# Scores of two heads in one planned step, planner durations reset, and low weight halves moved from an adding DMA to VectorE

## The chip, the core and the metric

The kernel runs on one core of one Trainium2 chip: TensorE (PE; its weight loads are listed as PEld), VectorE (DVE), ScalarE (ACT), GpSimd (POOL), SyncE (SP, which issues most transfers) and 16 DMA engines. The metric is the device time of one execution in microseconds (us), as the median of the runs.

## What is computed

Four batches of eight heads, 576 positions of 64 numbers each, go through attention of two kinds whose results are added; two dense layers follow over 2304 tokens of 512 numbers.

```python
q_d, k_d, v_d = means of 4 neighbouring positions          # 144 rows a head
out_up    = repeat(softmax(q_d @ k_d.T / 8) @ v_d, 4)       # attention over the means
out_local = softmax(where(|i-j| < 4, q @ k.T / 8, -1e9)) @ v
x = (out_up + out_local) as (2304, 512)
x = leaky(x @ moe_w_in, 0.01) @ moe_w_out                   # 512 -> 2048 -> 512
g(h) = h if h >= 1; 0 if h <= -1; else (h + 1)**2 / 4
return g(x @ moe2_w_in) @ moe2_w_out
```

## The kernel before

**Dense layers.** Every matrix is kept as a sum of two float16 parts, a high and a low one, and a product is three matmuls (high by high, high by low, low by high). Tokens go in five blocks (512, 512, 512, 512, 256); hidden columns go in 16 chunks of 128. A *step* is one chunk: 12 matmuls of 128x512 for the first layer (`g1`, L1456), ScalarE and VectorE work that makes the two parts of the activation (`act_a` L1472 or L1476, `act_s` L1480, `act_g` L1484, `act_h` L1496, and `act_l`, L1500 on VectorE), then 12 matmuls for the second layer (`g2`, L1521 in the first dense net, L1533 in the second). The blocks run in `ORDER`: blocks 0 and 1 of net 1, 0 and 1 of net 2, 2 and 3 of net 1, and so on. L1500 runs once a step (with two chunks a step in the small block, 144 times), so the n-th L1500 marks a place in the program.

**Weights.** `weight` brings each of 64 chunks (32 for each net) as raw 8-byte words, turns them into float32 on VectorE (L565, L572, L579), rounds to the high part on ScalarE (L595) and makes the low part. For net 1 the low part is one VectorE instruction (L628). For net 2, `LO_DMA` sends it another way: ScalarE writes the negated high part (L616), a DMA issued by GpSimd adds it onto the float32 value (L619), and ScalarE rounds the sum (L623).

**Attention over the means.** `down(b, hp, due)` runs for a batch and a pair of heads, 16 chains in all. For batches 0 and 1 the means of q and k come from sums over loaded and transposed tiles; for batches 2 and 3 from loads, adding DMAs issued by GpSimd (L828), an addition on VectorE (L835) and transposes on PE (L865, L869). Then `scores(par)` (L878) makes 2 matmuls of 72x144 in float32 for each head `par` of the pair, into that head's own PSUM bank; `peak` (L892) and `pexp` (L900) follow; `rec`, `norm` (L919), transposes (L929, L937) and `av` (L947, L955) end the chain. In the trace a float32 matmul has two records, so one `scores(par)` shows as x4.

**Local attention.** Tokens 0 to 1023 go through PE (`local_p`: L1022, L1037, L1050, L1055, L1080, L1097, after `prep`, whose transposes are L755). The rest goes through VectorE (`local_d`, five units: L1232, L1240, L1277, L1307), with transposes L1313 at the end.

**The order.** Nothing is scheduled by hand. Every piece of work is an `Op` with an engine, an assumed duration, dependencies, SBUF need, PSUM banks and a key (a due step less a lead). `Issue.run` plays the whole program through on assumed durations: whenever an engine is free it emits the ready op of the lowest rank, so the durations decide the order in which each engine's instructions are written. On the chip each engine runs its list in that order and waits on semaphores. The dense layers hold six of the eight banks while they run. Until the first dense matmul, whenever PE would have nothing ready, the planner writes a matmul over zeros into its list (`fill`, L1658, 0.216 us by its own count); afterwards it writes none. `pe_tr` gives the assumed time of a set of transposes, `pe_mm` of a set of matmuls, `t_dve` and `t_act` of one instruction, and `lat` is the flight of a transfer.

Of the kernel before, what the change touches and what calls it, by code (L numbers as in the profile page):

```python
# [45 lines left out]
D_ACT = (0, 0)  # L46
D_ACT_OF = {3: (2, 2)}

LO_DMA = {1: (99, 99), 2: (0, 99)}


LO_PE = (0, 0)
# [267 lines left out]
def kernel(  # L320
# [11 lines left out]
    nc = tc.nc  # L332
    B, H, S, D = q.shape
# [62 lines left out]

    def pe_tr(n, k, rows):

        return dict(dur=k * (0.003 + 2 * n / 2400.0), cols=k * 2 * n * rows / 128.0)

    def pe_mm(dur, n, k, rows):

# [4 lines left out]

    STEP = 5.2
    DMA = 0.47


    ident = const.tile([P, P], F32, name="ident")
# [122 lines left out]
    def weight(m, which, f, due):  # L535
# [49 lines left out]
            st["s"].free()  # L585
            w_open[0] -= 1

        o = ch.op("SP", DMA, load, need=(1024,), lat=1.55)
        o.gate = lambda: w_open[0] < AHEAD and (
            m == 1 or w_begun[1] == 2 * KFF and o.key <= sch.step + WINDOW_W and arena.close_spare()  # L590
        )
# [116 lines left out]
    def prep(b, hp, due):  # L708
# [67 lines left out]
        ch.rush, ch.window = RUSH_B.get(b, RUSH), WINDOW_B.get(b, WINDOW_A)  # L776
        ld = {}
        for nm, src in (("q", q), ("k", k)):
            ld[nm] = ch.op("SP", 2 * DMA, lambda nm=nm, src=src: load(nm, src), [],
                           need=(QBB * P,), lat=1.85)  # L780
        last = {}
        for nm in "qk":
# [7 lines left out]
                          after=(lambda nm=nm, i=i: banks.put(st["ps", nm, i]),))  # L790
            last[nm] = c
        n_v = 1 + (b == hp == 0) + (b == B - 1 and hp == NHP - 1)
        last["v"] = ch.op("SP", n_v * DMA, load_v, [], need=(2 * QBB * D,), lat=1.8)
        ch.close()
        last["load"] = ld["k"]
        prep_ready[b, hp] = last
# [2 lines left out]
    def down(b, hp, due):  # L799
# [46 lines left out]

        for nm, src in (("v", v),) if from_t else (("q", q), ("k", k), ("v", v)):
            o = ch.op("SP", DMA, lambda nm=nm, src=src: load(nm, src), [], need=(4 * rw * D,),
                      lat=rw * 0.42)
            if from_t:  # L850
                raw_v = o
            if whole:
                o = ch.op("Pool", 1.25, lambda nm=nm, src=src: more(nm, src), [o])
            else:
                o = ch.op("Pool", 1.05, lambda nm=nm, src=src: more(nm, src), [o], lat=0.85)
            pooled[nm] = ch.op("DVE", t_dve(256), lambda nm=nm: total(nm), [o], need=(4 * D,),
                               after=(lambda nm=nm: st["r" + nm].free(),))
# [12 lines left out]

        s_e = 1.0 / 16.0 if from_t else 1.0 / 128.0

        def scores(par):
            qk = st["qkT"].ap.rearrange("p (a g) -> p a g", a=2)
            st["ps_s", par] = banks.get()
            pp = slice(par * D, (par + 1) * D)
            for a in range(2):
                nc.tensor.matmul(  # L878
                    psv(par)[:, a, :], qk[pp, 0, a * GH:(a + 1) * GH], qk[pp, 1, :],
                    start=True, stop=True,  # L880
                )

        def psv(par):
            return st["ps_s", par][:GH, :2 * G].rearrange("p (a g) -> p a g", a=2)
# [75 lines left out]
        if from_t:  # L960
            r = prep_ready[b, hp]
            o = ch.op("DVE", t_dve(S), lambda: total_t("q"), [r["q"]], need=(2 * G,),
                      after=(qT[b, hp].done,))
            ch.op("DVE", t_dve(S), lambda: total_t("k"), [r["k"], o], after=(kT[b, hp].done,))
        else:
            ch.op("PE", pe_tr(GH, 4, GH), qk_t, [pooled["q"], pooled["k"]], banks=1,
                  after=(lambda: st["q"].free(), lambda: st["k"].free()))
            ch.op("ACT", t_act(288, True), qk_c, need=(2 * G,),
                  after=(lambda: banks.put(st["ps_t"]),))
        o = ch.ops[-1]  # L970
        e, x = None, None
        for par in range(2):
            o = ch.op("PE", pe_mm(0.49, G, 2, D), lambda par=par: scores(par), [o], banks=1,
                      after=(lambda: st["qkT"].free(),) if par else ())
            e = ch.op("DVE", 0.56, lambda par=par: peak(par), [o, e], need=() if par else (8,))
            x = ch.op("ACT", 2 * t_act(G, True, 2), lambda par=par: pexp(par), [e, x],
                      need=() if par else (4 * G,),
                      after=(lambda par=par: banks.put(st["ps_s", par]),))
# [3 lines left out]
        else:  # L982
# [6 lines left out]
                   after=(lambda: st["p"].free(),))  # L989
        c1 = ch.op("ACT", t_act(288, True), lambda: p_c(1), [t1, c0],  # L990
                   after=(lambda: banks.put(st["ps_p", 1]),))
        ch.op("PE", pe_mm(0.5, G, 4, GH), av, [c0, c1, pooled["v"]], banks=1,
              after=(lambda: st["v"].free(), lambda: st["pT"].free()))
        o = ch.op("ACT", t_act(144, True), av_c, need=() if hp else (NHP * G,), main=True,
                  after=(lambda: banks.put(st["ps_o"]),))
# [9 lines left out]
    def local_p(b, n0, cnt, hp, due):  # L1005
# [119 lines left out]
        def xl():  # L1125
# [3 lines left out]
            )  # L1129

        r = prep_ready[b, hp]
        ch.op("PE", pe_mm(0.12 + 0.172 * cnt, KB, 2 * cnt, D), scores, [r["q"], r["k"]], banks=1,
              after=(qT[b, hp].done, kT[b, hp].done))
        ch.op("DVE", t_dve(cnt * KB), peak, need=(2 * cnt,))
        ch.op("ACT", cnt * t_act(KB, True, 2), pexp, need=(cnt * KB,),
# [34 lines left out]
    def local_d(u, due):  # L1170
# [202 lines left out]
        for par in range(2):  # L1373
            reds = []
            mul = None
            for j0 in range(0, L, JC):
                end = j0 + JC == L
                o = mul = ch.op(
                          "DVE", big, lambda par=par, j0=j0: qk_mul(par, j0),
                          [ld["q", par], ld["k", par], mul],  # L1380
                          need=(JC * W * D,) + ((L * W,) if j0 == 0 else ()),
                          after=freer(*([("q", par), ("k", par)] if end else [])))
                if (par, j0) in q_act:
                    o = on_act(qk_red_act, par, j0, [o])
                    o.after = freer(("prod", par, j0))
                else:
                    o = ch.op("DVE", big, lambda par=par, j0=j0: qk_red(par, j0), [o],
                              after=freer(("prod", par, j0)))
                reds.append(o)
            o = ch.op("DVE", 0.685, lambda par=par: soft1(par), reds, need=(L,))  # L1390
            ex[par] = ch.op("ACT", t_act(56), lambda par=par: nc.scalar.activation(
                out=sv(par), in_=sv(par), func=AF.Exp, scale=0.125), [o])
            nrm[par] = ch.op("DVE", 0.815, lambda par=par: soft2(par), [ex[par]],
                             after=freer(("m", par)))
        fin = []
        done = {}
        for jh, j0 in enumerate(range(0, L, JC)):
            last = []
            for par in (1, 0) if (0, j0) in v_act else (0, 1):
                end = j0 + JC == L  # L1400
                if (par, j0) in v_act:
                    o = on_act(av_mul_act, par, j0, [nrm[par], ld["v", par]],
                               need=(JC * W * D,))
                else:
                    o = ch.op("DVE", big, lambda par=par, j0=j0: av_mul(par, j0),
                              [nrm[par], ld["v", par]], need=(JC * W * D,))
                o = done[par] = ch.op("DVE", t_dve(JC * 3 * D) + t_dve(JC * 2 * D) + t_dve(JC * D),
                                  lambda par=par, j0=j0: av_red(par, j0),
                                  [o, done.get(par)],
                                  need=Need(lambda: "o" in st, L * 2 * D),  # L1410
                                  after=freer(("prod", par, j0),
                                              *([("v", par), ("s", par)] if end else [])))
                last.append(o)
# [282 lines left out]
```

## Time and profile before

| | us |
|---|---|
| median of 3 runs (lowest, highest) | 875.11 (872.43, 875.77) |
| the profiled execution: its own time | 877.15 |
| its span, first to last instruction | 875.3 |
| PE busy | 865.7 (99%) |
| VectorE busy | 539.1 (62%) |
| ScalarE busy | 419.1 (48%) |
| GpSimd busy | 72.4 (8%) |
| mean granted TensorE clock | 0.994 |

Busy time of PE is to be read with care: matmuls overlap in their pipeline, so a group's length is best read from its start to the start of the next one. The shares are means over very different stages; VectorE at 62% is full in some stretches and nearly idle in the last half. An instruction on VectorE shows some 0.08 us that already overlaps with the next when both stand close together.

### The profile page before, as it was taken

The numbers are of one execution on the slowest core, as the hardware profiler recorded it, in microseconds if no ns is written. First come the engines' busy times: TensorE is split into PE (matmuls) and PEld (weight loads), VectorE is DVE, ScalarE is ACT, GpSimd is POOL, SyncE is SP. The second block draws the span as 40 slices with busy tenths as digits, with TensorE's granted clock in tenths as the row PEclk, the third lists the DMA queues.
The fourth block names the chain that finished last, engine by engine and source line by source line (L and its number), as shares of the span: only waits on it lengthen the run. The fifth ranks groups of instructions, "written<-read, shape, count | busy, mean of one in ns | idle before, by whom it ended". The sixth has DMA issues, their size and how long they took to land.

```text
span 875.3 us, 13271 instructions
## 1 busy us (share of the span) xinstructions
PE 865.7 (99%) x5014; PEld 446.0 (51%) x5014; DVE 539.1 (62%) x943; ACT 419.1 (48%) x973; POOL 72.4 (8%) x96
## 2 busy tenths in 40 slices
PE   9999999999999999999999999999999999999998
PEld 5765554444444444454444444444444488544564
DVE  5878999776679998848988955951322211322221
ACT  4878775677766433554444323222433332434343
POOL 2111000122210031100420000000000000000000
PEclk9999999999999998999999999999999999999999
DMA  8999466699984173312662004000000010000010
GB/s 149 163 189 219 154 205 189 157 254 237 245 205 105 23 173 48 90 43 67 115 136 71 1 1 109 0 1 1 1 1 0 1 50 1 1 1 1 0 49 24
DMA packets 84973, 76.07 MB, mean 87 GB/s; under 512 B 36910, under 2 KB 70574, under 8 KB 84910
## 3 DMA queue, kind: packets, MB, share of 16 engines
q1 hardware_dynamic: 69102, 62.69, 26.8%
q0 software_dynamic: 15808, 12.54, 9.7%
q8 instruction: 39, 0.64, 0.3%
q14 instruction: 24, 0.20, 0.1%
HBM read 62.08 MB, written 4.72 MB: 76 GB/s over the span
## 4 chain that ended last, share of the span: by engine, by line
PE 65%; DVE 3%; DMA 2%; ACT 1%; issue 1%; POOL 0%; POOLq 0%; SPq 0%; ACTq 0%
PE bank L1456 31%; PE bank L1533 20%; PE bank L1521 12%; DMA arena<-in_k_dram 1%; PE bank L878 1%; DMA arena<-arena 1%; DVE arena L1240 1%; PE bank L929 1%; PE bank L947 1%; PE bank L1313 1%; DVE arena L1307 0%; DVE arena L1500 0%; PE bank L865 0%; DVE arena L835 0%; DVE arena L579 0%
## 5 line engine op out<-in xcount | busy, mean ns | idle before, releaser
L1456 PE MATMUL bank<-arena,w 128*128 128x512 f16 (+1 forms) x1920 | 395.6, 358 | 0.3 <-DVE arena L1561 0.3
L1456 PEld LDWEIGHTS <-w 128*128 128x128 f16 x1920 | 186.6, 98 | 182.8 <-issue 1.6
L1533 PE MATMUL bank<-w,arena 128*128 128x512 f16 x864 | 201.1, 383 | 0.4 <-ACT arena L1496 0.2
L1521 PE MATMUL bank<-arena,w 128*128 128x512 f16 (+1 forms) x960 | 200.3, 360 | 0.0
L1500 DVE SCALAR_TENSOR_TENSOR arena<-arena 128x512 f16<-128x512 f32 x144 | 99.0, 688 | 140.1 <-ACT arena L1496 137.8
L1521 PEld LDWEIGHTS <-w 128*128 128x128 f16 x960 | 93.3, 98 | 91.4 <-issue 3.5
L1533 PEld LDWEIGHTS <-arena 128*128 128x128 f16 x864 | 84.3, 98 | 100.1 <-issue 4.0
L1484 DVE SCALAR_TENSOR_TENSOR arena<-arena,bank 128x512 f32<-128x512 f32 x72 | 49.2, 684 | 134.0 <-ACT arena L1480 134.0
L1496 ACT ACTIVATE arena<-arena 128x512 f16<-128x512 f32 x144 | 90.6, 629 | 80.3 <-DVE arena L1484 73.3
L1476 ACT ACTIVATE arena<-bank,half 128x512 f32<-128x512 f32 x72 | 49.2, 684 | 119.4 <-PE bank L1456 117.5
L1472 ACT ACTIVATE arena<-bank 128x512 f32<-128x512 f32 x72 | 42.6, 592 | 120.1 <-PE bank L1456 119.8
L1480 ACT ACTIVATE arena<-arena 128x512 f32<-128x512 f32 x72 | 45.3, 629 | 1.9
L1307 DVE TENSOR_TENSOR arena<-arena 128x768 f32<-128x768 f32 (+2 forms) x60 | 41.2, 688 | 1.4
L619 POOL DMA_DIRECT2D arena<-arena x32 | 27.8, 869 | 160.9 <-DVE arena L565 70.1
L1232 DVE TENSOR_TENSOR arena<-arena 128x1792 f32<-128x1792 f32 x20 | 40.3, 2017 | 1.0 <-DMA arena<-in_k_dram 0.5
L1240 DVE TENSOR_REDUCE arena<-arena 128x28 f32<-128x1792 f32 x20 | 40.2, 2008 | 0.0
L1277 DVE TENSOR_TENSOR arena<-arena 128x1792 f32<-128x1792 f32 x20 | 40.1, 2014 | 0.0
L623 ACT ACTIVATE w<-arena 128x512 f16<-128x512 f32 x32 | 20.0, 626 | 19.2 <-DMA arena<-arena 19.0
L595 ACT ACTIVATE w<-arena 128x512 f16<-128x512 f32 x34 | 21.1, 621 | 10.6 <-DVE arena L579 10.6
L579 DVE SCALAR_TENSOR_TENSOR arena<-arena 128x512 int32<-128x512 int32 x32 | 22.1, 689 | 0.7
L572 DVE SCALAR_TENSOR_TENSOR arena<-arena 128x512 int32<-128x512 int32 x32 | 22.0, 689 | 0.7
L595 ACT ACTIVATE w<-w 128x512 f16<-128x512 f32 x30 | 18.5, 627 | 7.9 <-DVE w L579 7.9
(138 smaller groups left out, 681.9 us busy)
## 6 DMA issues: line engine op xcount, KB each, us to landing
arena<-in_moe_w_in_dram SPq DMA_DIRECT2D x18, 512.0 KB
arena<-in_moe_w_out_dram SPq DMA_DIRECT2D x18, 512.0 KB
arena<-arena POOLq DMA_DIRECT2D x32, 256.0 KB, 5.7
w<-in_moe_w_in_dram SPq DMA_DIRECT2D x14, 512.0 KB
w<-in_moe_w_out_dram SPq DMA_DIRECT2D x14, 512.0 KB
out_dram<-arena SPq DMA_DIRECT2D x18, 256.0 KB
arena<-in_k_dram SPq DMA_DIRECT2D x23, 112.0 KB
arena<-in_v_dram SPq DMA_DIRECT2D x23, 112.0 KB
```

The costliest lines, as they stand in the source:

```text
L1232: nc.vector.tensor_tensor(pv(par, j0), st["q", par].ap.rearrange("p (j d) -> p j d", d=D)[:, j0:j0 + JC, :] .unsqueeze(2).to_broadcast([P, ...
L1240: nc.vector.reduce_sum(sv(par)[:, j0:j0 + JC, :], pv(par, j0), axis=AX)
L1307: nc.vector.tensor_tensor(out, x, y, op=ALU.add)
L1456: nc.tensor.matmul(h[:, e], a[:, f, c, :], y[:, :, c, :], start=(n == 0), stop=(n == 3 * KDM - 1),)
L1472: nc.scalar.activation(out=t, in_=st["h", p], func=AF.Prelu, scale=s_in * sg, alpha=0.01)
L1476: nc.scalar.activation(out=t, in_=st["h", p], func=AF.Relu, scale=0.5 * s_in, bias=half)
L1480: nc.scalar.activation(out=t, in_=t, func=AF.Square, scale=s_in ** -0.5)
L1484: nc.vector.scalar_tensor_tensor(out=t, in0=t, scalar=1.0 / s_in, in1=st["h", p], op0=ALU.min, op1=ALU.max)
L1496: nc.scalar.activation(out=gv(p)[0], in_=st["t", p].ap, func=AF.Copy, scale=so)
L1500: nc.vector.scalar_tensor_tensor(out=lo, in0=st["t", p].ap, scalar=so, in1=hi, op0=ALU.mult, op1=ALU.subtract)
L1521: nc.tensor.matmul(o, a, y[:, e, :], start=(first and n == 0 and c % E == 0), stop=(last and n == 2), skip_group_check=True,)
L1533: nc.tensor.matmul(st["acc"][tt], a, y[:, f, :], start=(first and n == 0), stop=(last and n == 2),)
```

## The change

- **Scores.** `scores(par)`, planned twice for each chain of `down` with one bank each, becomes `scores()`, planned once with two banks. It writes the same four matmuls, now alternating between the heads. The two heads stand on partitions 0 to 63 and 64 to 127, and write different banks. `peak` and `pexp` of both heads depend on the one op.
- **Assumed durations.** Transposes get 0.06 us more a set, the scores of `local_p` and `av` of `down` a little more, loads of q and k 1.35 in place of 0.94, weight loads a flight of 1.75 in place of 1.55, and a few VectorE ops and flights are reset.
- **Low parts.** `LO_DMA` no longer selects any chunk, so the low parts of all 32 chunks of net 2 are made by the VectorE instruction (L628, L629 after).

```diff
-LO_DMA = {1: (99, 99), 2: (0, 99)}
+LO_DMA = {1: (99, 99), 2: (99, 99)}
...
-        return dict(dur=k * (0.003 + 2 * n / 2400.0), cols=k * 2 * n * rows / 128.0)
+        return dict(dur=0.06 + k * (0.003 + 2 * n / 2400.0), cols=k * 2 * n * rows / 128.0)
...
+    T_SC = 0.75
...
-        o = ch.op("SP", DMA, load, need=(1024,), lat=1.55)
+        o = ch.op("SP", DMA, load, need=(1024,), lat=1.75)
...
-            ld[nm] = ch.op("SP", 2 * DMA, lambda nm=nm, src=src: load(nm, src), [],
+            ld[nm] = ch.op("SP", 1.35, lambda nm=nm, src=src: load(nm, src), [],
...
-        def scores(par):
+        def scores():
             qk = st["qkT"].ap.rearrange("p (a g) -> p a g", a=2)
-            st["ps_s", par] = banks.get()
-            pp = slice(par * D, (par + 1) * D)
+            for par in range(2):
+                st["ps_s", par] = banks.get()
             for a in range(2):
-                nc.tensor.matmul(
-                    psv(par)[:, a, :], qk[pp, 0, a * GH:(a + 1) * GH], qk[pp, 1, :],
-                    start=True, stop=True,
-                )
+                for par in range(2):
+                    pp = slice(par * D, (par + 1) * D)
+                    nc.tensor.matmul(
+                        psv(par)[:, a, :], qk[pp, 0, a * GH:(a + 1) * GH], qk[pp, 1, :],
+                        start=True, stop=True,
+                    )
...
+        o = ch.op("PE", pe_mm(T_SC, G, 4, D), scores, [o], banks=2,
+                  after=(lambda: st["qkT"].free(),))
         e, x = None, None
         for par in range(2):
-            o = ch.op("PE", pe_mm(0.49, G, 2, D), lambda par=par: scores(par), [o], banks=1,
-                      after=(lambda: st["qkT"].free(),) if par else ())
...
-        ch.op("PE", pe_mm(0.5, G, 4, GH), av, [c0, c1, pooled["v"]], banks=1,
+        ch.op("PE", pe_mm(0.64, G, 4, GH), av, [c0, c1, pooled["v"]], banks=1,
...
-        ch.op("PE", pe_mm(0.12 + 0.172 * cnt, KB, 2 * cnt, D), scores, [r["q"], r["k"]], banks=1,
+        ch.op("PE", pe_mm(0.15 + 0.178 * cnt, KB, 2 * cnt, D), scores, [r["q"], r["k"]], banks=1,
...
-            o = ch.op("DVE", 0.685, lambda par=par: soft1(par), reds, need=(L,))
+            o = ch.op("DVE", 0.8, lambda par=par: soft1(par), reds, need=(L,))
```

Below, line numbers after the change are 1 to 4 higher (L878 becomes L882, L628 L629, L1500 L1504, L1658 L1662). Between the marks, the lists of all engines change order, since every duration enters the plan.

PE, before the first dense matmul (L1037 and L878 are scores, L755 and L929 transposes, "zeros" the fill), in the list before:

```order
L1037 MATMUL bank_68<-w_61 64x70 x8
L755 MATMUL bank_66<-ident,w_61 128x64 x5
L878 MATMUL bank_70<-w_61 72x144 x2
L755 MATMUL bank_64<-ident,w_61 128x64 x4
L929 MATMUL bank_65<-ident,w_61 72x72 x4
L878 MATMUL bank_69<-w_61 72x144 x2
L929 MATMUL bank_67<-ident,w_61 72x72 x4
L1028 LDWEIGHTS ident_72
```

and after:

```order
L1041 MATMUL bank_69<-w_61 64x70 x8
L882 MATMUL bank_66<-w_61 72x144
L882 MATMUL bank_67<-w_61 72x144
L882 MATMUL bank_66<-w_61 72x144
L882 MATMUL bank_67<-w_61 72x144
L756 MATMUL bank_70<-ident,w_61 128x64 x5
L756 MATMUL bank_64<-ident,w_61 128x64 x4
L933 MATMUL bank_65<-ident,w_61 72x72 x4
L1032 LDWEIGHTS ident_72
```

The two sets of scores of a chain, which stood apart with transposes between them, are one run of four that alternates between two banks.

PE, inside net 2's first blocks, at the first chain of batch 2 (L1533 is a dense matmul with its weight load), in the list before:

```order
L1533 LDWEIGHTS arena
L1533 MATMUL bank_63<-w_61,arena 128x512
L878 MATMUL bank_68<-arena 72x144 x2
L865 MATMUL bank_69<-ident,arena 128x72 x4
L1533 LDWEIGHTS arena
L1533 MATMUL bank_70<-w_61,arena 128x512
```

and after:

```order
L1537 LDWEIGHTS arena
L1537 MATMUL bank_66<-w_61,arena 128x512
L882 MATMUL bank_65<-arena 72x144
L882 MATMUL bank_68<-arena 72x144
L882 MATMUL bank_65<-arena 72x144
L882 MATMUL bank_68<-arena 72x144
L1537 LDWEIGHTS arena
L1537 MATMUL bank_67<-w_61,arena 128x512
```

Dense work is interrupted once for both heads, where the second head's scores used to wait for a later gap 12 dense matmuls on.

VectorE, while net 1 works on blocks 0 and 1 (L565, L572, L579: conversion of a weight chunk; L1500: `act_l`), in the list before:

```order
L565 TENSOR_SCALAR arena<-arena 128x512
L572 SCALAR_TENSOR_TENSOR arena<-arena 128x512
L1500 SCALAR_TENSOR_TENSOR arena<-arena 128x512
L579 SCALAR_TENSOR_TENSOR arena<-arena 128x512
L565 TENSOR_SCALAR arena<-arena 128x512
L572 SCALAR_TENSOR_TENSOR arena<-arena 128x512
```

and after:

```order
L566 TENSOR_SCALAR arena<-arena 128x512
L573 SCALAR_TENSOR_TENSOR arena<-arena 128x512
L629 SCALAR_TENSOR_TENSOR w_61<-arena,w_61 128x512
L580 SCALAR_TENSOR_TENSOR arena<-arena 128x512
L566 TENSOR_SCALAR arena<-arena 128x512
L573 SCALAR_TENSOR_TENSOR arena<-arena 128x512
L629 SCALAR_TENSOR_TENSOR w_61<-arena,w_61 128x512
L1504 SCALAR_TENSOR_TENSOR arena<-arena 128x512
```

L629 joins every chunk of net 2, in the same list as `act_l`, on which the next `g2` of PE waits.

## Rows read from the trace of the kernel before

**Rows 1.** The page, engines: busy us (share of the span) and instructions.

```profile
PE 865.7 (99%) x5014; PEld 446.0 (51%) x5014; DVE 539.1 (62%) x943; ACT 419.1 (48%) x973; POOL 72.4 (8%) x96
```

**Rows 2.** Windows, cut at the first dense matmul and at the 4th, 14th, 36th L1500.

```profile
core 0: us, PE busy (x) PEld busy (x) DVE busy (x) ACT busy (x) POOL busy (x), PEclk, DMA share, GB/s
0.00:60.70 60.70, 59.50 (x657) 40.66 (x658) 43.12 (x135) 40.66 (x176) 11.29 (x31) 1.00 0.95 164
60.70:78.20 17.50, 17.08 (x115) 9.05 (x113) 13.64 (x32) 15.60 (x60) 2.50 (x4) 1.00 1.02 189
78.20:157.50 79.30, 78.88 (x558) 41.16 (x559) 76.41 (x168) 54.21 (x160) 1.42 (x3) 0.98 0.60 182
157.50:274.70 117.20, 116.86 (x542) 52.84 (x541) 84.13 (x142) 83.12 (x150) 26.11 (x30) 1.00 0.89 222
274.70:330.30 55.60, 52.92 (x248) 24.00 (x246) 53.10 (x69) 23.46 (x41) 10.21 (x9) 0.99 0.42 87
```

**Rows 3.** Waits of PE over the whole run: us in total, times, longest.

```profile
PE bank L865 <- DVE arena L835: 2.7, 2, 2.5
```

**Rows 4.** Timeline of PE, 330 to 356: start, us, instructions [idle before].

```profile
329.98 0.50 PE L865 MATMUL bank<-ident,arena 72*128 72x72 f32 x2 [2.51 <-DVE arena L835]
330.28 5.33 PE L1533 MATMUL bank<-w,arena 128*128 128x512 f16 x12
...
336.71 2.75 PE L1533 MATMUL bank<-w,arena 128*128 128x512 f16 x12
339.40 0.71 PE L878 MATMUL bank<-arena 64*72 64x144 f32 x4
340.04 2.76 PE L1533 MATMUL bank<-w,arena 128*128 128x512 f16 x12
...
355.08 0.71 PE L947 MATMUL bank<-arena 72*64 72x144 f32 x8
355.73 0.47 PE L865 MATMUL bank<-ident,arena 72*128 72x72 f32 x4
```

**Rows 5.** Timeline of PE, 155 to 170.

```profile
160.44 2.75 PE L1521 MATMUL bank<-arena,w 128*128 128x512 f16 x12
...
165.62 2.75 PE L1521 MATMUL bank<-arena,w 128*128 128x512 f16 x12
```

**Rows 6.** Timeline of PE, 0 to 61.

```profile
1.20 5.46 PE L1658 MATMUL bank<-zeros 128*128 128x512 bf16 x16 [1.20 <-DVE half L429]
...
57.23 0.71 PE L1037 MATMUL bank<-w 64*64 64x70 f32 x16
57.87 0.46 PE L755 MATMUL bank<-ident,w 64*128 64x64 f32 x4
...
60.72 7.93 PE L1456 MATMUL bank<-arena,w 128*128 128x512 f16 x36
```

**Rows 7.** Waits on all engines from 0 to 60.7, two of the longest.

```profile
ACT w L768 <- PE bank L755: 9.5, 5, 5.1
DVE w L1050 <- PE bank L1037: 5.3, 7, 1.1
```

**Rows 8.** VectorE by line, 78.2 to 157.5: busy us, mean ns | idle before.

```profile
L628 DVE SCALAR_TENSOR_TENSOR w<-w,w 128x512 f16<-128x512 f32 x25 | 16.9, 683 | 0.0
```

**Rows 9.** Timeline of VectorE, 155 to 170.

```profile
156.25 0.68 DVE L579 SCALAR_TENSOR_TENSOR arena<-w,arena 128x512 int32<-128x512 int32 x1
156.85 0.68 DVE L1500 SCALAR_TENSOR_TENSOR arena<-arena 128x512 f16<-128x512 f32 x1
...
161.93 0.69 DVE L1500 SCALAR_TENSOR_TENSOR arena<-arena 128x512 f16<-128x512 f32 x1 [2.55 <-ACT arena L1496]
```

**Rows 10.** VectorE by line, 157.5 to 274.7.

```profile
L579 DVE SCALAR_TENSOR_TENSOR arena<-arena 128x512 int32<-128x512 int32 x31 | 21.4, 689 | 0.7
L1500 DVE SCALAR_TENSOR_TENSOR arena<-arena 128x512 f16<-128x512 f32 x23 | 15.8, 688 | 20.7 <-ACT arena L1496 20.7
L1232 DVE TENSOR_TENSOR arena<-arena 128x1792 f32<-128x1792 f32 x2 | 4.0, 2018 | 0.0
```

More of the change, by code (lines that the diff above doesn't have):

```diff
@@ L792, in prep @@
         n_v = 1 + (b == hp == 0) + (b == B - 1 and hp == NHP - 1)
-        last["v"] = ch.op("SP", n_v * DMA, load_v, [], need=(2 * QBB * D,), lat=1.8)
+        last["v"] = ch.op("SP", n_v * DMA, load_v, [], need=(2 * QBB * D,), lat=1.0 + 0.95 * n_v)
         ch.close()
@@ L848, in down @@
             o = ch.op("SP", DMA, lambda nm=nm, src=src: load(nm, src), [], need=(4 * rw * D,),
-                      lat=rw * 0.42)
+                      lat=0.45 * rw)
             if from_t:
@@ L965, in down @@
         else:
-            ch.op("PE", pe_tr(GH, 4, GH), qk_t, [pooled["q"], pooled["k"]], banks=1,
+            ch.op("PE", pe_mm(0.5, GH, 4, GH), qk_t, [pooled["q"], pooled["k"]], banks=1,
                   after=(lambda: st["q"].free(), lambda: st["k"].free()))
@@ L1406, in local_d @@
                               [nrm[par], ld["v", par]], need=(JC * W * D,))
-                o = done[par] = ch.op("DVE", t_dve(JC * 3 * D) + t_dve(JC * 2 * D) + t_dve(JC * D),
+                o = done[par] = ch.op("DVE", 2.05,
                                   lambda par=par, j0=j0: av_red(par, j0),
```

## The prediction

> **What bounds the kernel now.** I read the engines line first: PE is busy 99% of the span, VectorE 62%, ScalarE 48% [rows 1]. The time is therefore PE's list, and a microsecond is won by a shorter list or by one of PE's few gaps. The windows by stage come second, because the means hide where another engine is close behind PE [rows 2]. In the ramp, up to 60.7, PE does transposes, scores and fills (matmuls over zeros) and no dense work. From 78.2 to 157.5 VectorE is busy 76.4 of 79.3 us, so two engines are full at once. From 157.5 to 274.7 it is busy 84.1 of 117.2 us and has room; from 274.7 to 330.3 it is full again, 53.1 of 55.6. Third, the waits: the largest stall of PE that a line names is L865 waiting for the addition L835, 2.7 us, of which one wait is 2.5 [rows 3]. The timeline shows what it costs besides [rows 4]: the 12 dense matmuls after it take from 330.28 to about 335.6, 5.33 us, where the same 12 take 2.59 from start to start elsewhere (160.44 to 165.62 holds 24 of them, so 5.18 [rows 5]). That is the level of 1.2 GHz in place of 2.4, granted after a wait of 2.5 us; wait and half clock together cost some 5.3.
>
> Those 5.18 us are a step, and 22 steps need 114.0 us of PE with nothing between them.
>
> **Merged scores.** A visit to the scores of one head, 2 matmuls of 144 columns, costs 0.64 us (339.40 to 340.04), and some 0.10 more on entering, as the 12 dense matmuls ahead of it take 2.69 (336.71 to 339.40) and not 2.59 [rows 4]: 0.74. The merged visit has four matmuls. No row of before shows two matmuls of 64 rows on the two halves of the array together. If the pairs overlap, the visit for both heads is as long as one for one head, 0.64; if they run one after another, it is twice 0.64, or somewhat less where a fixed part falls away, so 1.12 to 1.28 (the 0.16 is an estimate, a quarter of a visit). Nearest rows: `av` L947, 4 matmuls of 144 columns on two column halves, takes 0.65 (355.08 to 355.73) [rows 4], and L1037, 8 matmuls of 70 columns over both row and column halves, 0.64 (57.23 to 57.87) [rows 6]. These are 576 and 560 columns in the time of the lone visit's 288, so matmuls on different parts of the array do overlap there. L1037 takes both halves of the rows as the merged scores do, so I take 0.64, and a chain saves 0.74. At the serial bound it saves 1.48 - 1.22 = 0.26 at best, 0.10 at worst.
>
> The lone row of L878, doubled, says 1.28. The Trainium skill, TensorEngine Tiling (Array Packing), section Tiling Modes, says that different tiles load weights and multiply in parallel; by it the visit takes 0.64, by the doubled row 1.12 to 1.28, and the sum below would be 864.5 by the one and 869.9 by the other. Its section Restrictions and Gotchas adds that row tiles may not use one PSUM bank at the same time; the new op has two banks. No run so far shows two 64x128 tiles together.
>
> Of 16 chains 5 lie ahead of the first dense matmul, 3 between 60 and 125, and 8 (batches 2 and 3) from 330 on.
>
> **The ramp.** The new list has 39 fills where the old has 50: two more in the first run (16 at 1.20 to 6.59, 0.34 each [rows 6]) and 13 fewer later, at 0.216 each. That is 2.8 less some 0.4, so 2.4 us. Five merged chains take off 5 x 0.64 = 3.2. Five transposes move behind the first dense matmul: 0.4. At most 6.0. At least 0: if the loads or the other engines set the end of the ramp, PE waits for what it no longer does; the DMA engines show a share of 0.95 there [rows 2]. For PE as the bound speaks that the others wait for it in the ramp, ScalarE 9.5 us for transposes and VectorE 5.3 for L1037 [rows 7], while PE is idle for only 1.2 of its 60.7 us [rows 2], and that at the very start [rows 6]; against it, fills hide waits. I take 4.2, so the first dense matmul starts at about 56.5. The three chains behind it save 3 x 0.74 = 2.2. Together 6.4, between 2.2 and 8.2.
>
> **What VectorE lets through.** L629 takes 0.68 [rows 8], but instructions that stand close begin 0.61 apart (156.25 to 156.85, at the same size [rows 9]), so I count 0.61. The 4th to the 14th `act_l`: by such a count the list of before needs 79.3 us, which is all of the stretch, and the new one 80.7 (one weight chunk fewer, other work moved in). So 1.4 of the lead is lost. The 14th to the 36th: 31 of L629 are 18.9 us; six more large ops of `local_d` are 6 x 1.93 = 11.6 (2.02 each [rows 10], less the overlap of 0.08); one more conversion 1.2 (two instructions like L579 [rows 10]); `av_red` and `soft` of the moved units some 3.0. In all 34.5. On top of the 81.6 counted for the old list, or the 84.1 of the windows [rows 2], that is 116 to 119 us, where PE's 22 steps need 114.0 and the stretch took 117.2. VectorE passes from room to full. It doesn't stop PE at once: `act_l` that begins at 161.93 ends at 162.62 [rows 9], and the `g2` that reads it starts at 165.62 [rows 5], so 3.0 us of delay are free. But the 20.7 us for which VectorE waits for ScalarE ahead of L1500 [rows 10] go. The stretch gives between 1.2 won and 1.8 lost. From a lead of 6.4: 6.4 - 1.4 + 1.2 = 6.2 down to 6.4 - 1.4 - 1.8 = 3.2; from 2.2, -1.0. The list has pieces that are uneven (the fourth to the fifth `act_l` hold 22.1 us of VectorE work, 12.9 before), so I take the low end, **3.0 gained by 274.7**.
>
> ScalarE loses 64 instructions (L616, L623) and GpSimd's queue 32 adding transfers of 256 KB. Their cover: from 157.5 to 274.7 PE is idle for 0.3 us in all and ScalarE is busy for 83 of 117 [rows 2], so I cost this at nothing on PE's side; it only makes `act_h` earlier, on which L1500 waits. If that cover were gone, less work on ScalarE could still not lengthen PE's list.
>
> **The stall at L865.** In the new list the first set of L866 stands one step (5.2 us) earlier against dense work, and so does the addition ahead of it on VectorE: its place in the list does not decide whether PE waits. It is decided by the loads and GpSimd's adding DMAs (L828) behind which VectorE waits; the 32 L619 ahead of these in GpSimd's queue are gone, and flights are assumed longer. VectorE is as full in 274.7 to 330.3 as before by count (56.5 against 56.8 to the 48th `act_l`). From 0 to 5.5 are won; I take half, **2.7**.
>
> **Eight chains in the dense part.** Nothing but PE bounds it from 356 on, so 8 x 0.74 = **5.9** (serial: 2.1).
>
> **New waits** of PE where VectorE is full, above all at the fourth and fifth `act_l`, with some half clock after them: 0 to 5, I take **1.0** lost, the size of the small gaps of the old list (PE's idle of 0.4 and 0.3 in the two stretches [rows 2]) and as much half clock.
>
> **Sum.** -3.0 - 2.7 - 5.9 + 1.0 = -10.6. The profiled execution had a span of 875.3 in a time of 877.15; the median is 875.11, 2.04 under that execution. I take the sum from the median: **864.5**.
>
> **The rivals.**
> *Scores in a row.* The pairs don't overlap. The eight chains give 2.1 in place of 5.9; the eight others give 8 x 0.48 = 3.8 less, of which VectorE would have eaten more than half, so 1.6: -10.6 + 3.8 + 1.6 = -5.2, 869.9. For it: the only visit of this form takes 0.64 for 288 columns. Against it: L1037.
>
> *VectorE eats the lead.* Its lists run at the pace of its windows without slack: 79.3 + 1.4 + 2 in the first full stretch and 120.5 in the second, which leaves nothing of the lead at 274.7, and the stall stays: -5.9 + about 1.7 of new waits (an estimate: four small ones of 0.4, the idle that the stretches from 78.2 and from 157.5 show [rows 2]), -4.2, 870.9.
>
> *VectorE becomes the bound (slower).* Place: 157.5 to 274.7 and the stretch behind it, where L629 stands in VectorE's list ahead of `act_l`, on which `g2` waits, and behind `g2` all of PE's list. Price: each wait of 2.5 us brings 2.6 of half clock, as at 330 [rows 4], so 5.1 each. Three such (15.3) and the stall kept against -5.9 and the lead of 3.0 give +6.4: 881.5. It decides when VectorE needs more than 117.2 + 3.0 + 3.0 = 123 us for those 22 steps, 5% above my count.
>
> *The reset durations change nothing at L865*: the forecast and 2.7 more, 867.2, inside its own range.
>
> **How the numbers follow.** Forecast 0.62 (857 to 870), scores in a row 0.12, the lead eaten 0.14, slower 0.12. The lower end: all of the ramp and the stall (6.2 + 5.5 + 5.9 = 17.6, 857.5). The upper end is above the two middle rivals and leaves out the slower one: 857.0 to 873.0. A measurement tells about 0.5%, 4.4 us, from no change, so faster is below 870.7: nearly all of the forecast (0.58), part of the first rival (0.07) and of the second (0.05), 0.70; same 0.04 + 0.05 + 0.09 = 0.18, and slower 0.12.
>
> **What would show it.** L882 as one visit x8 of 0.64 to 0.75 in the dense part (1.2 if the rival holds). First dense matmul near 56.5. VectorE busy 116 to 119 us between the 14th and the 36th L1504, with 31 of L629, and little idle ahead of L1504. L866 without a wait of 2 us and no 12 matmuls at 5.3 behind it. The forecast is wrong if PE's waits name L1504 or a low part with more than 5 us in all, or if the ramp ends at 60 again.

## The result, and the profile after

The changed kernel takes 867.24 us (median of 6 runs, 863.81 to 868.97); the kernel before took 874.98 in the same comparison. The ratio is 0.9908, 95% interval 0.9888 to 0.9927: 8.0 us less. On two other chips the same kernel stood at 0.9870 (0.9851 to 0.9889) and 0.9870 (0.9837 to 0.9903), some 11 us less. The profiled execution has a span of 864.4 in a time of 866.15, against 875.3 in 877.15 before, so the two profiles differ by 11.0 us and the medians by 7.7: the profiled execution of before is slower than all others of its kernel in this comparison (875.77 at most), and that of after is a little faster than its median. A gain read by laying the two profiles side by side is therefore some 3 us larger than the gain of the medians.

The page of the kernel after, its head, and the windows cut at the first dense matmul and at the 4th, 14th and 36th L1504, as in [rows 2]:

```profile
span 864.4 us, 13078 instructions
PE 853.9 (99%) x5001; PEld 442.2 (51%) x5003; DVE 552.2 (64%) x975; ACT 386.6 (45%) x909; POOL 44.5 (5%) x64
...
0.00:60.10 60.10, 57.27 (x639) 41.08 (x642) 41.04 (x131) 40.83 (x180) 11.29 (x31) 0.91 0.90 160
60.10:80.90 20.80, 19.60 (x128) 9.91 (x127) 14.27 (x38) 17.32 (x61) 2.50 (x4) 0.95 0.88 173
80.90:160.20 79.30, 76.88 (x550) 39.71 (x551) 77.32 (x169) 52.49 (x154) 1.68 (x3) 0.98 0.62 193
160.20:274.70 114.50, 114.50 (x532) 51.91 (x531) 113.78 (x191) 53.77 (x92) 0.00 (x0) 1.00 0.52 155
274.70:330.30 55.60, 55.60 (x270) 25.61 (x268) 52.80 (x72) 22.23 (x42) 7.12 (x6) 1.00 0.33 69
```

Three things stand in it. The ramp is as long as before (60.1 against 60.7), but its mean clock is 0.91. From 160 to 275 VectorE is full, 113.8 of 114.5 us, and yet PE has no idle time there. From 275 to 330 PE's 2.7 us of idle are gone.

The waits of PE over the whole run (us in total, times, longest), without those of the ramp:

```profile
PE bank L1525 <- ACT w L596: 1.4, 2, 1.1
...
PE bank L756 <- ACT w L904: 1.1, 1, 1.1
...
PE bank L933 <- ACT w L904: 0.7, 1, 0.7
...
PE bank L1525 <- DVE w L629: 0.5, 2, 0.3
PE bank L1537 <- ACT arena L1500: 0.2, 1, 0.2
```

The stall of [rows 3] is gone, and in its place PE waits six times soon after the ramp, between 60 and 100, for weights whose high part (L596) or low part (L629) is not ready and for `pexp` (L904). PE's timeline where the stall of [rows 4] was:

```profile
323.75 0.42 PE L866 MATMUL bank<-ident,arena 72*128 72x72 f32 x4
324.01 2.75 PE L1537 MATMUL bank<-w,arena 128*128 128x512 f16 x12
326.69 0.71 PE L882 MATMUL bank<-arena 64*72 64x144 f32 x8
327.34 2.76 PE L1537 MATMUL bank<-w,arena 128*128 128x512 f16 x12
```

L866 starts without a wait, the 12 dense matmuls behind it run at full clock, and a merged visit for both heads takes 0.65 us (326.69 to 327.34), what one head took before.

Where the time went is best seen by counting dense matmuls, of which every kernel here has the same 3744. The table gives the time at which n of them are done and the next one starts, worked out from PE's timeline, less the same time before (minus is earlier):

| dense matmuls done (time before) | after | after, 2nd chip | after, 3rd chip |
|---|---|---|---|
| 0, the first starts (60.7) | -0.6 | -4.8 | -4.5 |
| 96 (94.1) | +5.0 | +1.7 | +0.3 |
| 240 (137.9) | +2.7 | -0.6 | -2.0 |
| 792 (258.9) | +2.7 | -0.6 | -2.0 |
| 1080 (321.6) | +2.4 | -0.9 | -2.3 |
| 1176 (352.4) | -3.9 | -7.2 | -8.6 |
| the last starts (871.3) | -11.0 | -14.3 | -14.6 |

The gain of the ramp is lost by the 96th; nothing happens from the 240th to the 792nd; where the stall was, between the 1080th and the 1176th, 6.3 come back, two merged chains among them; the six chains behind bring 6.0 to 7.1.

### The profile page after: what moved, and what is told of

It reads as the page before. It is cut to its first block, busy times and chain, and to the rows that moved or that the text cites. A ratio compares the mean times of both kernels' runs of the same rounds, so it can differ in the third digit from the quotient of the medians.

```text
span 864.4 us, 13078 instructions
## 1 busy us (share of the span) xinstructions
PE 853.9 (99%) x5001; PEld 442.2 (51%) x5003; DVE 552.2 (64%) x975; ACT 386.6 (45%) x909; POOL 44.5 (5%) x64
## 4 chain that ended last, share of the span: by engine, by line
PE 96%; DVE 2%; ACT 1%; issue 1%; DVEq 0%; ACTq 0%
PE bank L1460 43%; PE bank L1537 21%; PE bank L1525 21%; PE bank L1101 1%; PE bank L951 1%; PE bank L882 1%; PE bank L756 1%; PE bank L1041 1%; PE bank L933 1%; PE bank L1662 1%; PE bank L1095 1%; PE bank L1084 1%; PE bank L1317 1%; DVE w L629 0%; PE bank L1026 0%
## 5 line engine op out<-in xcount | busy, mean ns | idle before, releaser
L1537 PE MATMUL bank<-w,arena 128*128 128x512 f16 x864 | 198.5, 379 | 0.4 <-ACT arena L1500 0.2
L1504 DVE SCALAR_TENSOR_TENSOR arena<-arena 128x512 f16<-128x512 f32 x144 | 99.0, 687 | 125.4 <-ACT arena L1500 125.1
L1500 ACT ACTIVATE arena<-arena 128x512 f16<-128x512 f32 x144 | 90.6, 630 | 65.9 <-DVE arena L1488 64.2
L596 ACT ACTIVATE w<-arena 128x512 f16<-128x512 f32 x34 | 21.3, 628 | 34.7 <-DVE arena L580 34.5
L829 POOL DMA_DIRECT2D arena<-in_q_dram x8 | 11.8, 1472 | 296.8 <-DMA arena<-in_k_dram 208.7
L596 ACT ACTIVATE w<-w 128x512 f16<-128x512 f32 x30 | 18.8, 629 | 16.4 <-DVE w L580 16.4
L629 DVE SCALAR_TENSOR_TENSOR w<-arena,w 128x512 f16<-128x512 f32 x34 | 23.1, 681 | 0.0
```

The source lines that it names most:

```text
L1500: nc.scalar.activation(out=gv(p)[0], in_=st["t", p].ap, func=AF.Copy, scale=so)
L1504: nc.vector.scalar_tensor_tensor(out=lo, in0=st["t", p].ap, scalar=so, in1=hi, op0=ALU.mult, op1=ALU.subtract)
L1537: nc.tensor.matmul(st["acc"][tt], a, y[:, f, :], start=(first and n == 0), stop=(last and n == 2),)
```

## The experiments

Figures "under before" are differences of medians within one comparison. Kernels of one group of four ran on one chip.

**The changed kernel again.** The first profile has a clock of 0.91 in the ramp. Is that its list, or that execution?

> The changed kernel once more, nothing edited. Theory A (the 11 fills that the new list lacks let the clock fall to half in the ramp): the profile again shows a granted clock near 0.5 for some 10 us or more between 45 and 65 us, the first dense matmul at 58 to 61, median 865 to 869. Theory B (the half clock of the first profile was one execution's accident): granted clock 1.00 in that stretch, first dense matmul at 54 to 56.

862.88 (861.13 to 865.12), 10.9 under before. The clock windows of the first profile, 40 to 48.7, 48.7 to 62.4 and 62.4 to 76 (columns as in [rows 2]):

```profile
40.00:48.70 8.70, 8.12 (x98) 5.77 (x96) 7.51 (x24) 5.91 (x21) 0.19 (x2) 1.00 1.10 186
48.70:62.40 13.70, 13.70 (x115) 10.22 (x116) 7.85 (x23) 7.65 (x32) 1.47 (x3) 0.50 0.81 160
62.40:76.00 13.60, 13.13 (x95) 6.76 (x92) 9.45 (x21) 11.11 (x37) 2.50 (x4) 1.00 0.88 179
```

and the middle one in this run:

```profile
48.70:62.40 13.70, 13.70 (x141) 8.71 (x141) 10.27 (x27) 10.16 (x43) 2.29 (x6) 1.00 0.87 180
```

In the first, PE is busy all of 13.7 us and gets the level of 1.2 GHz; in the second, 2.4. The same list does both: theory B holds for this run. Ahead of the fall PE had been busy from 41.5 on, behind a gap of 0.57 us; in the second run its last gap, 0.43 us, is at 36.5. The first dense matmul starts at 55.92, where the prediction had 56.5. Which executions have the half clock is asked below.

**Ten more fills in the ramp.**

```diff
                     best.fn()
+                    if e == "PE" and fill is not None and kept_at + 4.0 <= t < 58.0:
+                        kept_at = t
+                        for _ in range(2):
+                            fill(t)
                     end = t + best.dur
```

> The changed kernel with ten more matmuls over zeros, in pairs about 4 us apart between 31 and 58 us of the ramp; everything else stays in its order. They cost 10 x 0.216 = 2.2 us of PE. Theory A (too few fills, half clock): clock 1.00 through the ramp, first dense matmul at 55 to 58, median 861 to 865, some 4 below the changed kernel. Theory B (the ramp's end is set by loads and other engines, or the clock falls anyway): first dense matmul at 60 or later, median 867 to 870.

862.08 (859.01 to 867.12), 0.8 below the changed kernel in the same group, so within its spread. The profiled execution, the slowest of the six, has the half clock all the same, from 50.6 to 64.3:

```profile
50.60:64.30 13.70, 13.04 (x113) 10.14 (x116) 6.27 (x15) 5.92 (x25) 1.47 (x3) 0.50 0.84 159
```

Ten fills do not exclude it. Theory A has the median, but not the clock and not the gain of 4; the profiled execution (first dense matmul at 63.73) goes as theory B says. Ten fills that would cost 2.2 us left the median no higher: no run shows what a fill costs.

**The kernel before without its last six fills.**

```diff
+        if t < 24.0:
-        nc.tensor.matmul(
+            nc.tensor.matmul(
```

> The kernel before without its last six fills (those behind 27 us of the ramp), nothing else. They cost 6 x 0.216 = 1.3 us of PE. Theory A (fills keep the clock): granted clock near 0.5 for 8 us or more between 45 and 65 us, median 877 to 881. Theory B (fills only wait): 873 to 874.5, clock 1.00.

873.71 (869.72 to 878.35) where before has 873.79 (ratio 1.0004, 0.9986 to 1.0021): no change in the median, so theory B by its number. One of twelve executions, the profiled one, has the half clock from 53.3 to 67.0 and is the slowest. The kernel before shows a mean clock of 0.994 or more in all 46 executions that these comparisons hold.

This profile also shows the stall of [rows 3] a second time, and without the half clock behind it:

```profile
333.93 0.35 PE L865 MATMUL bank<-ident,arena 72*128 72x72 f32 x2 [2.17 <-DVE arena L835]
334.15 2.75 PE L1533 MATMUL bank<-w,arena 128*128 128x512 f16 x12
```

In the profile of before, the clock over the same place is

```profile
329.20:336.00 6.80, 6.02 (x16) 2.39 (x17) 5.61 (x10) 2.22 (x5) 2.37 (x2) 0.50 0.82 118
```

So a wait of 2.2 us cost 2.2 here, where in the other execution a wait of 2.5 came with 6.8 us of half clock; PE worked through 6.0 of these, which cost some 3 us more.

**Merged scores alone.** The kernel before with `scores()` of the diff, assumed at 0.75; durations and adding DMAs as before.

> The kernel before with the merged scores alone (assumed 0.75 for the op); durations and the adding DMAs stay as before. Theory A (the pairs overlap, one visit of 0.64 saved for each of 16 chains, all of it kept behind 330): 8 x 0.74 = 5.9 there and a part of the eight others, median 866 to 869. Theory B (the gain of the chains ahead of 330 is eaten and the stall stays or grows): 869 to 872. If the pairs ran in a row: 872 to 874.

860.98 (859.62 to 862.99): 12.8 under before, more than the changed kernel in the same group (10.9), and more than either theory. Its first dense matmul starts 3.1 earlier; at the 792nd it has 4.3 of lead, at the 1176th 9.4, at the last 14.2. The wait at L865 has shrunk from 2.5 to 1.0 (timeline of PE), and no half clock follows:

```profile
325.05 0.35 PE L865 MATMUL bank<-ident,arena 72*128 72x72 f32 x2 [1.03 <-DVE arena L835]
325.23 2.76 PE L1535 MATMUL bank<-w,arena 128*128 128x512 f16 x12
```

**Low parts on VectorE alone.** The kernel before with the line `LO_DMA` of the diff.

> The kernel before with the low parts of net 2 on VectorE alone (no adding DMAs of weights); scores and durations as before. Theory A (it fills VectorE from 157 to 275, and PE has no lead to lose): PE waits for L628 or L1500 between 157 and 275, the stall at L865 stays, median 873 to 878. Theory B (it frees GpSimd's queue, so that the addition L835 comes in time and the stall at L865 goes): no wait of over 1 us at L865, median 868 to 872.

868.95 (868.55 to 869.40): 5.4 under before, and the five runs lie within 0.85 us where those of before spread over 5.8. The largest of PE's waits (whole run) are now

```profile
PE bank L1658 <- DVE half L429: 1.2, 1, 1.2
PE bank L929 <- ACT w L1055: 0.4, 1, 0.4
```

The stall is gone; theory B. By dense count nothing else moves much: +1.0 at the first, -0.9 at the 1080th, -6.4 at the 1176th. GpSimd's first L828 is issued at 314.12, against 320.54 before. But in the kernel with the merged scores alone, which keeps the adding DMAs, it is issued at 313.14, so the 32 L619 ahead of it do not by themselves make it late.

**Reset durations alone.** The kernel before with all of the diff's numbers, scores apart, adding DMAs kept.

> The kernel before with the reset durations alone; scores apart, adding DMAs as before. It has 36 fills where before has 50. Theory A (the ramp gets some 3 us shorter but VectorE, full from 78 to 157, eats that; the stall may go): median 870 to 874. Theory B (the durations carry most of the gain): 864 to 868. With the clock at half in the ramp, 875 or more.

871.19 (870.99 to 873.01), 3.1 under before. The stall is gone here too (L865 at 322.99, no wait), but by the 240th dense matmul the kernel is 2.0 behind before, having been 2.4 ahead at the first: it waits there for weights (1.7 us for L595, 0.7 for L628), and its clock is at half for 6.8 us from 81.5 on. Theory A has the number.

**The changed kernel with the adding DMAs back.**

> The changed kernel with the adding DMAs put back: merged scores and reset durations, low parts as before. The changed kernel stood 10.9 under before in the last comparison, the merged scores alone 12.8. Theory A (moving the low parts costs and gains nothing, as PE is not behind VectorE): 10 to 12 under before. Theory B (the low parts on VectorE are what the changed kernel loses against the merged scores alone): 13 to 15 under before. Theory C (they help, and the durations cost): 7 to 9 under before.

867.57 (864.28 to 873.22), 6.8 under before, on a chip on which four of its six executions have a mean clock of 0.993 or less; the fastest two, at 0.998 and 0.993, are 10.1 and 9.7 under. The profiled one has the half clock from 48.3 to 62.0. The median is nearest to theory C, just outside its 7 to 9, but not by its mechanism: by dense count, half-clock profile against half-clock profile, this kernel is 0.8 us behind the changed one at the end. I take the verdict as open within that spread; the pair with the old durations, below, bears on it again.

**Scores head by head.** In the changed kernel:

```diff
-            for a in range(2):
-                for par in range(2):
+            for par in range(2):
+                for a in range(2):
```

> The changed kernel with the four matmuls of the merged scores written head by head (both of the first head, then both of the second) instead of alternating; the plan and all other instructions stay as they are. Theory A (neighbours overlap only where they stand on different halves of the array): the visit grows from 0.64 to between 0.9 and 1.28, 16 visits, 0.3 to 0.6 each on PE, median 3 to 9 above the changed kernel, so 2 to 8 under before. Theory B (the order doesn't matter): visit of 0.64 to 0.7, median within 1.5 of the changed kernel, 9.5 to 12.5 under before.

The visit, in PE's timeline:

```profile
322.42 0.72 PE L882 MATMUL bank<-arena 64*72 64x144 f32 x8
323.07 2.76 PE L1537 MATMUL bank<-w,arena 128*128 128x512 f16 x12
```

0.65, against 0.64 alternating (323.41 to 324.05 in the second run of the changed kernel). Theory B holds for the visit: the order does not matter. In both orders the eight records start in pairs some 0.01 us apart. The median, 866.34 (861.16 to 873.30, 12 executions), is 8.0 under before and misses theory B's 9.5 to 12.5; it is spread by the half clock: five executions have a mean clock of 0.992 or less (865.5 to 873.3). The changed kernel itself was not run on this chip. The profiled one, at 0.998, has a span of 861.8, 0.7 more than the changed kernel's 861.1.

**Merged scores and low parts, old durations.**

> Merged scores and low parts on VectorE, with the old durations (49 fills). Merged scores alone stood 12.8 under before, the low parts alone 5.4. Theory A (both remove the same stall at L865, which can go only once): 12 to 14 under before, the low parts add nothing. Theory B (the two gains add up): 16 to 18 under. Theory C (the low parts make VectorE late once the ramp is shorter): 8 to 11 under, with waits of PE for L630 or L1502 between 78 and 275.

860.32 (859.46 to 860.93): 13.0 under before, ratio 0.9845 (0.9814 to 0.9876). Merged scores alone were 12.8 under, on another chip: the low parts add 0.2, theory A. With the intervals of the two ratios (0.9832 to 0.9868, 0.9814 to 0.9876) a gain or loss of up to some 3 us would not be seen. The head of its page:

```profile
span 858.3 us, 13049 instructions
PE 849.2 (99%) x5009; PEld 438.3 (51%) x5013; DVE 552.2 (64%) x975; ACT 385.8 (45%) x909; POOL 43.8 (5%) x64
```

and the largest waits of PE, whole run:

```profile
PE bank L1082 <- ACT arena L902: 1.2, 1, 1.2
PE bank L1660 <- DVE half L429: 1.2, 1, 1.2
PE bank L1523 <- DVE w L628: 0.6, 1, 0.6
```

The first dense matmul is 3.1 ahead of before, 1.4 less than in the changed kernel of this group, but at the 96th it is 5.4 ahead, where the changed kernel is 0.3 behind. By dense count, less before, with the two parts alone beside it:

| dense matmuls done | merged scores alone | low parts alone | both, old durations |
|---|---|---|---|
| 0, the first starts | -3.1 | +1.0 | -3.1 |
| 96 | -5.4 | -0.3 | -5.4 |
| 240 | -5.6 | -0.3 | -5.6 |
| 792 | -4.3 | -0.3 | -4.3 |
| 1080 | -3.1 | -0.9 | -4.9 |
| 1176 | -9.4 | -6.4 | -11.9 |
| the last starts | -14.2 | -8.2 | -17.5 |

The last two columns differ by the merged scores alone. From the 1080th on these bring 5.4 (12.6 against 7.3), with no half clock in either and the idle time of PE equal to 0.1 us: 0.67 for each of eight chains. The first and the third column differ by the low parts alone, and these two profiles by 3.4 at the end, 2.6 of it from waits of 1.6 (L1535 for L1563) and 1.0 (L865) that the third column does not have. The profiled execution of the first is its slowest, so the medians need not differ as much.

The clock after the ramp, from the fourth to the fourteenth `act_l`, in the second run of the changed kernel and here:

```profile
76.00:156.90 80.90, 77.19 (x550) 39.13 (x551) 77.45 (x168) 52.60 (x154) 1.32 (x3) 0.98 0.61 192
75.10:154.10 79.00, 76.29 (x557) 39.30 (x558) 77.30 (x171) 53.82 (x161) 1.31 (x3) 1.00 0.56 180
```

The 0.98 is one stretch of 3.4 us at half clock (86.7 to 90.1), just after PE's wait of 2.1 for L596. Every profile with all or some of the reset durations has such a stretch between 74 and 90 us (the durations alone 6.8 us), and so has the kernel before (80.0 to 83.5); those of merged scores alone, low parts alone and both have none.

**The changed kernel a third time**, as the measure for this group.

> The changed kernel, nothing edited, on the chip of these four runs, as the measure for the other three. By its runs so far 8 to 11 under before, with a granted clock of 0.994 or less in some executions.

862.29 (861.25 to 865.20), 11.0 under. Its fastest run is slower than the slowest of the kernel with the old durations. At the 240th dense matmul its profile is 3.6 behind that kernel's: PE has idled 1.7 longer by then, and the 3.4 us of half clock cost another 1.7.

**Only the 0.06 for transposes.** Merged scores, low parts on VectorE, and `dur=0.06 + ...` in `pe_tr`; 37 fills.

> Merged scores, low parts on VectorE, and of all reset durations only the 0.06 us more for a set of transposes (37 fills; without it the list has 49). Theory A (this one number takes the fills out and, with them, opens the ramp to the half clock and brings the first dense matmuls ahead of their weights): like the changed kernel, 8 to 11 under before, with PE waiting over 1.5 us in all for L595 or L628 between 60 and 95. Theory B (the other durations are what costs): like the kernel with the old durations, 12 to 14 under.

860.34 (859.53 to 870.99), 13.0 under before. The five executions at 859.5 to 860.6 are as fast as those with the old durations, though PE has a wait of 3.0 in the ramp's wake:

```profile
PE bank L1523 <- ACT w L595: 3.0, 1, 3.0
```

The sixth, 870.99, has a mean clock of 0.981. Theory A falls for the median: 12 fills fewer cost nothing there.

**All durations but that one.**

> The changed kernel without the 0.06 us more for a set of transposes, all other reset durations kept (45 fills). Theory A: 12 to 14 under before, few executions with a clock under 0.995. Theory B (the others cost): 8 to 11 under, as the changed kernel.

861.55 (859.74 to 863.63), 11.8 under before, all six with a clock of 0.997 or more. It lies between the two theories, 0.7 below the changed kernel and 1.2 above the one with the old durations, within the spread of both. By dense count it is 6.3 ahead at the first and 1.3 behind at the 96th, as the changed kernel is: so what loses the lead of the ramp seems to be in the other durations, weight loads, q and k loads, scores, `av` or VectorE's, and which one was not tried.

**The half clock, counted.** An execution with the half clock of 13.7 us in the ramp has a mean clock of 0.993 or less in the four profiles that show one (0.990, 0.990, 0.990, 0.992). By that mark, which the executions without a trace cannot confirm:

| kernels | fills | executions at 0.993 or less |
|---|---|---|
| old `pe_tr`: before, merged alone, low parts alone, both, all durations but `pe_tr` | 45 to 50 | 0 of 66 |
| new `pe_tr`: after (three times), DMAs back, head by head, `pe_tr` alone, durations alone | 36 to 39 | 13 of 47 |
| before less six, after with ten more | 44, 49 | 1 of 12, 1 of 6 |

It goes with the new `pe_tr`, whose list in the ramp is shorter and has fewer fills; the third line says that the number of fills alone doesn't decide. What does, and why chips differ (after: 2 of 6, 0 of 5, 1 of 6), stays open. Nor does the half clock make the first comparison slower than the later two: three of its executions, with mean clocks of 0.994 and 0.996, took 868.3 to 869.0, where the later two have 862 to 865 at 0.996.

## Right or wrong, step by step

The forecast was 864.5, range 857 to 873. Measured: 867.2 in the first comparison, 862.9 and 862.3 in the later ones. The sign, the size and the range held; the sum was right partly by luck. By dense count the two later profiles gain 14.3 and 14.6, not 10.6: the lead was taken too large, the stall and the chains brought more together than was forecast. The medians gain 11 because they are not counted from the slow profile of before, from which the prediction read the prices of its sum.

- **Merged visit: right.** 0.64 taken, 0.64 to 0.65 measured, so matmuls on the two halves of the rows do run together. The trace agrees here with the Trainium skill, TensorEngine Tiling (Array Packing), section Tiling Modes, which says that different tiles can load weights and multiply in parallel. The reading of L1037 [rows 6] was the right neighbour, doubling the lone row of L878 the wrong one. The alternation is no condition for it.
- **Ramp: the mechanism right, its clock missed.** 56.5 was forecast; 55.9 and 56.2 came in two profiles, 60.1 in the first, with 13.7 us at half clock. A ramp that ends at 60 again was named as a sign that the forecast is wrong; in that one execution it came, and by the clock. Merged scores alone bring the first dense matmul forward by 3.1, where 3.2 was forecast for them. I had priced the fills as pure waste, 2.4 us; neither run that adds or leaves out fills shows a cost in its median.
- **VectorE's full stretches: the wrong place.** 116 to 119 us of VectorE work were forecast for the 22 steps; 113.8 busy came, 2 to 5 less. PE lost nothing from the 240th to the 792nd dense matmul, so the slack of 3.0 us read from [rows 5] and [rows 9] covers a full VectorE. The lead was lost earlier, from the first to the 96th, where the prediction expected merged chains to add to it (2.2 up to 125 us) and allowed 1.0 for new waits, put down to a full VectorE: PE idles 4.5 us longer there in the second profile than before (6.1 more in all by the 96th, 1.7 of them in the ramp), 2.7 of it named as L596, 1.8 as L904. In these lists a ramp that ends earlier meets weights that have not been converted; with the old durations it ends 3.1 earlier and keeps its lead. The forecast kept 3.0 of the lead at 275; 0.6 and 2.0 remained in the clean profiles, and 2.7 were lost in the first.
- **Stall at L865: undersized.** I took half of 5.5 because its place in the list didn't decide it; it went whole, 6.3 between the 1080th and the 1176th, two chains' scores included, and 5.4 there with the low parts alone, which is also what these gain in the medians. The price of 5.3 was read from one execution with 6.8 us of half clock. 30 of 46 executions of before have a mean clock of 0.998 or more, which by an estimate (twice the missing share of 875 us) leaves room for some 4 us of it; how those lose as much was not seen. Each of the three parts removes it alone (merged scores leave 1.0), so it was a near miss in one plan and not the price of any of them. The parts alone give 12.8, 5.4 and 3.1, in sum 21, together 8 to 11: the stall can go only once. How early L828 is issued for these chains goes with it (320.5 before, 300.6 to 314.5 in the kernels without it or with less of it); what decides that wasn't tried.
- **Eight chains: about right.** 5.9 forecast, 5.4 between the two kernels that differ by the merged scores alone.
- **ScalarE and GpSimd at nothing: not contradicted.** Merged scores with and without the adding DMAs differ by 0.2, on two chips and within some 3 us.

Of the rivals, *scores in a row* fell with the visit. *VectorE becomes the bound* fell with 114.5 us of PE without idle. *VectorE eats the lead* had the outcome for the lead (not much left at 275) and the wrong cause, and it kept the stall, which went. *The reset durations change nothing at L865* has the first median almost to the digit, 867.2, and is wrong all the same: with the durations alone L865 starts without a wait.

So the three parts, by the runs: merged scores carry nearly all of it, the low parts add nothing on top that these runs can tell, and the reset durations cost about 2 us (860.3 against 862.3 on one chip, no overlap) and go with the half clock in some executions. The kernel with the diff's scores and low parts and the old durations has the lowest median and is among the steadiest of those run; it beats before and after. Merged scores alone (861.0) and the new `pe_tr` alone (860.34) are as fast within their spread.

## What to carry to other kernels

Price a stall that a plan has by accident apart from the edits, and from more than one execution: any edit that moves the plan may remove it, and it cannot be won twice. When a phase ahead of a bound engine is shortened, ask first what the next phase's inputs are waiting for, not only how full the engines are on average. Resetting assumed durations did not by itself make a better order here.

## What was not expected of the hardware

TensorE got the half clock for 13.7 us while the profile shows it busy without a gap, in a stretch made up mostly of small float32 transposes and matmuls of 64 to 72 rows or columns; the same list got the full clock in other executions. A wait of PE of 2.5 us was followed by the half clock in one execution, one of 2.2 us at the same place in nearly the same list was not. Four matmuls of 64 rows in two halves take 0.65 us head by head and 0.64 alternating, as long as two on one half.
